# An FFT mixing layer fused with a two-layer MLP: another layout for the block transposes, later slots, another start

## The chip, the cores and the metric

The kernel runs on one core of a Trainium2 chip. The core's engines work side by side, each through its own list of instructions in order: TensorE (PE) for matrix products into PSUM, VectorE (DVE), ScalarE (ACT), GpSimd (POOL) and SyncE (SP); POOL and SP here mostly issue DMAs. The metric is the time of one execution on the device in microseconds (us), lower is better. Three runs of the kernel before took 919.62, 919.73 and 919.87 us.

## The reference

Each of 8 batches holds 3008 rows of 256 numbers. Along the rows it is transformed by a real FFT, multiplied by a filter of 1505 complex frequencies for each column, and transformed back. All 24064 rows then go through two dense layers with a leaky ReLU between them.

```python
X = np.fft.rfft(x, axis=1)                       # x: 8 x 3008 x 256
Y = X * (filt_r + 1j * filt_i)[None, :, :]       # 1505 x 256
y = np.fft.irfft(Y, n=x.shape[1], axis=1)
h = y.reshape(8 * 3008, 256) @ w_in              # 256 x 2048
g = np.maximum(0.01 * h, h)
out = g @ w_out                                  # 2048 x 256, float32
```

## The kernel before, in words

**The transform.** 3008 = 94 x 32 (`N1`, `N2`), so the FFT is done as two rounds of small products with constant matrices, with a transposition between them, and the same backwards. All operands are fp16. For one batch:

- *s1* (`s1_group`, 16 groups of two): for each of 32 values of n2, 94 rows of x meet a 94 x 128 matrix (`f1_sb`, twiddle factors included). The result is [128 frequencies, 32, 256]; ACT copies it from PSUM to the buffer `big` (line 205).
- *T1* (`turn`, four parts): DVE transposes 32 x 32 blocks, that is, it swaps the position within each group of 32 partitions with the index of n2 (line 212). It moves two fp16 numbers as one 32-bit element. A part covers 32 of the 128 such pairs in a row, with all 32 values of n2: 1024 elements a partition. In the buffer a row is laid out as (32, 256), so neighbouring elements of a block lie 512 B apart, in the source and in the destination.
- *s2* (`s2_group`, 12 groups): products with the 128 x 128 matrix `fwd2`, then the filter. In batch 0 (`split`), DVE makes two products y1, y2 and PE adds them in the next step. In the other batches DVE makes three products (lines 238 to 240) and POOL adds them (line 242).
- *sa* (`sa_group`): the inverse of s2, copied to `big` by ACT (line 255). *T2* (`turn`): the transposition back. *sb* (`sb_group`, 16 groups): products with `i1_sb`, which DVE copies into `yts` (line 272), already transposed for the dense layers.

Three `big` buffers go round; s1 of one batch, T1, sa and T2 write them in turn. All PSUM tiles of the transform (s1, s2, sa, sb) come from one pool, `pfp`, with two buffers, given out in the order of the program.

**The dense layers.** Rows are taken in 47 chunks of 512. A chunk has 8 slots. In a slot, `moe1_group` makes four products of 512 columns for 256 of the 2048 inner columns, and ACT writes their leaky ReLU (line 296); `moe2_slice` makes eight products of 256 columns for the chunk before (line 304). Every fourth slot the finished output, 128 x 512 in fp32, is copied from PSUM by DVE (line 308) and sent out by SP.

**The order.** It is written out by hand: nothing is moved by the framework, which only adds the waits that data and buffers need. Batch 0 is transformed ahead of everything else. The loop at the end then runs over 376 slots and 8 more; `plan` puts the transform groups of batches 1 to 7 into slots, behind the slot's `moe1_group` and ahead of its `moe2_slice`. Batch b starts at slot 47 (b - 1) - 8 (batch 1 at slot 0), and one batch is 47 slots of the dense layers. Within a batch: s1 in slots 0 to 7, T1 in 8 and 9, s2 from 11 on and sa from 15 on, each at 5/4 slots for a group, T2 in 30 and 31, sb in 32 to 39.

**The start.** SP issues the loads of the constants; POOL those of x, the filters, the weights and the next x, all of which turn fp32 into fp16 on the way. Each POOL DMA waits until the one eight places before it has landed. The filters are loaded into partitions 0 to 63 of `fa_sb` and `fb_sb`, and DVE copies them to 64 to 127, once as they are and once negated (lines 341, 342). One row of the filter (the highest frequency) overwrites a row of the copy by a DMA of its own (line 344). DVE also zeroes the three `big` buffers (line 190).

Of the kernel before, what the change touches and what calls it, by code (L numbers as in the profile page):

```python
# [23 lines left out]
def _build_np_constants(N):  # L24
# [68 lines left out]
    return (fwd1.astype(np.float16), inv1.astype(np.float16), small.astype(np.float16))  # L93
# [3 lines left out]
def kernel(  # L97
# [27 lines left out]
    f1_sb = cpool.tile([P, N2, P], FP16, name="f1_sb")  # L125
# [7 lines left out]
    big = [cpool.tile([P, Q, D], FP16, name=f"big{i}") for i in range(3)]  # L133
# [36 lines left out]
    def filt_load(dst, src):  # L170
        h = N2 // 2
        for s in range(2):
            q = s * Q
            nc.gpsimd.dma_start(dst[q : q + h], rows(src, NC * s, N1, 1, h, NC))

            nc.gpsimd.dma_start(
                dst[q + h : q + Q, 1 - s : NC - s],
                rows(src, N1 - (1 - s) - NC * s, N1, -1, h, NC - 1),
            )
        nc.gpsimd.dma_start(dst[h:Q, 0:1], rows(src, N1 // 2, N1, 1, h, 1))  # L180


    nc.sync.dma_start(f1_sb[:, 0:16, :], f1_d.ap()[:, 0:16, :])
    nc.sync.dma_start(f1_sb[:, 16:32, :], f1_d.ap()[:, 16:32, :])
# [13 lines left out]
    def s1_group(b, g):  # L198
        def go():
            ps = pfp.tile([P, 2, D], FP32, tag="pf", name=f"s1_b{b}_g{g}")  # L200
            for j in range(2):
                n2 = 2 * g + j
                nc.tensor.matmul(ps[:, j, :], f1_sb[:N1, n2, :], x_sb[:N1, n2, :],  # L203
                                 start=True, stop=True)
            nc.scalar.copy(big[(4 * b) % 3][:, ds(2 * g, 2), :], ps[:])  # L205
        return go

    def turn(src, dst, i, parts):
        w = D // 2 // parts
        a = src[:].bitcast(FP32)[:, :, ts(i, w)].rearrange("p n e -> p e n")  # L210
        o = dst[:].bitcast(FP32)[:, :, ts(i, w)].rearrange("p n e -> p e n")
        nc.vector.transpose(o, a)  # L212

# [5 lines left out]
    def s2_group(b, g, split):  # L219
        def go():  # L220
            src = big[(4 * b + 1) % 3]
# [7 lines left out]
            if split:  # L229
                y1 = ypp.tile([P, 2, D], FP16, tag="y", name=f"y1_b{b}_g{g}")  # L230
                y2 = ypp.tile([P, 2, D], FP16, tag="y2", name=f"y2_b{b}_g{g}")
                nc.vector.tensor_tensor(y1[:], ps[:], fa, AL.mult)
                nc.vector.tensor_tensor(y2[:], ps[:], fb, AL.mult)  # L233
                ys[(b, g)] = (y1, y2)
            else:
                p1 = scrp.tile([P, 2, D], FP32, tag="p1", name=f"p1_b{b}_g{g}")
                p2 = scrp.tile([P, 2, D], FP32, tag="p2", name=f"p2_b{b}_g{g}")
                nc.vector.tensor_tensor(p1[:], ps[:], fa, AL.mult)  # L238
                nc.vector.tensor_tensor(p2[0:64], ps[64:P], fb[64:P], AL.mult)  # L239
                nc.vector.tensor_tensor(p2[64:P], ps[0:64], fb[0:64], AL.mult)  # L240
                y1 = ypp.tile([P, 2, D], FP16, tag="y", name=f"y_b{b}_g{g}")
                nc.gpsimd.tensor_tensor(y1[:], p1[:], p2[:], AL.add)  # L242
                ys[(b, g)] = (y1,)
        return go

    def sa_group(b, g):
        def go():
# [7 lines left out]
            nc.scalar.copy(big[(4 * b + 2) % 3][:, ds(2 * g, 2), :], ps[:])  # L255
# [5 lines left out]
    def sb_group(b, g):  # L261
        dt, h = g % 2, g // 2

        def go():
            src = big[(4 * b + 3) % 3]
# [6 lines left out]
            nc.vector.tensor_copy(yv[:, :, ds(4 * h, 4)], ps[:].rearrange("p c a -> p a c"))  # L272
# [124 lines left out]
```

## Time and profile before

| | |
|---|---|
| Time, median of three runs | 919.73 us |
| The profiled execution's own time | 919.45 us |
| its span, first to last instruction | 917.6 us |
| mean granted TensorE clock | 0.972 of full speed |
| busy: PE, ACT, DVE, POOL | 799.3, 496.6, 464.6, 127.2 us |
| batch 0's transform alone, until the first dense product | 0 to 88.1 us |
| transposes (64) | 135.1 us busy on DVE |

A line of the page's groups reads: line of the kernel, engine, operation, what it writes <- what it reads, partitions x elements, count | busy us, mean ns of one | idle time of the engine before it, and what ended most of that. In the chain of waits and in the timeline, a line begins with its start and its duration in us. In the view by stretches a line gives the stretch, its length, the busy time of PE, weight loads, DVE, ACT and POOL with the number of instructions in brackets, then the granted clock, the share of the DMA engines and GB/s. Buffer numbers are left out of names: `s_b_g` is the PSUM tile of an s1 or s2 group, `sa_b_g`, `sb_b_g` those of sa and sb, `h_c_g` and `o_c_t` those of the two dense layers. The page's line on the granted clock and its neighbours (40 slices of the span):

```profile
PE   3065799889989898998989898998989898999998
DVE  5467386538650785329661676319661586400011
PEclk9999989999999998999999999999989999899999
```

### The profile page before, as it was taken

Reading aid. Unit: us, or ns where it says so; the run is one execution under the profiler, and the core shown is the slowest. Engines: PE = TensorE matmul, PEld = TensorE weight load, DVE = VectorE, ACT = ScalarE, POOL = GpSimd, SP = SyncE. Lnnn points to the kernel's source line nnn. Section 1 sums busy time; section 2 is a strip of 40 time slices with the busy share of each in tenths; the row PEclk is TensorE's granted clock in tenths of the full one; section 3 lists DMA queues with packets and bytes.
Section 4 is the critical chain, followed back from the end, with each engine's and each line's share of the span. In section 5 each row is a group of like instructions: output and inputs, shape, how many; then the busy total and the mean of one; then the engine's idle time right before and its main releaser. Section 6 shows DMA issues by size and latency. Waiting matters only on the chain.

```text
span 917.6 us, 13333 instructions
## 1 busy us (share of the span) xinstructions
PE 799.3 (87%) x5725; PEld 537.2 (59%) x5725; DVE 464.6 (51%) x571; ACT 496.6 (54%) x602; POOL 127.2 (14%) x123
## 2 busy tenths in 40 slices
PE   3065799889989898998989898998989898999998
PEld 1013456665667655785657655775656665667666
DVE  5467386538650785329661676319661586400011
ACT  4021756474637564585647565585636665455553
POOL 4100042003200240003300141003300041000000
PEclk9999989999999998999999999999989999899999
DMA  9900301041001400122101400013001001011011
GB/s 204 178 0 1 68 24 35 24 91 36 35 24 35 97 30 24 35 67 59 36 24 35 102 24 35 35 45 82 24 35 35 24 24 35 24 47 35 35 42 52
DMA packets 31707, 43.49 MB, mean 47 GB/s; under 512 B 2166, under 2 KB 29910, under 8 KB 30926
## 3 DMA queue, kind: packets, MB, share of 16 engines
q0 software_dynamic: 5504, 15.98, 10.3%
q1 hardware_dynamic: 26144, 26.66, 8.3%
q8 instruction: 45, 0.74, 0.4%
q14 instruction: 14, 0.11, 0.0%
HBM read 33.97 MB, written 24.64 MB: 64 GB/s over the span
## 4 chain that ended last, share of the span: by engine, by line
PE 68%; DVE 20%; DMA 4%; ACT 4%; issue 3%; POOL 0%; DVEq 0%; ACTq 0%; POOLq 0%
PE o_c_t L304 30%; PE h_c_g L291 28%; DVE big L212 12%; PE sb_b_g L269 3%; PE s_b_g L227 3%; DMA fa_sb<-in_filt_r_dram 3%; PE sa_b_g L253 2%; PE s_b_g L203 2%; DVE p_b_g L240 2%; DVE p_b_g L239 2%; DMA x_sb<-in_x_dram 2%; DVE p_b_g L238 2%; ACT gt_c L296 2%; ACT big L205 1%; DVE ost_c_t L308 1%
## 5 line engine op out<-in xcount | busy, mean ns | idle before, releaser
L296 ACT ACTIVATE gt_c<-h_c_g 128x1024 f16<-128x1024 f32 x376 | 385.8, 1026 | 355.9 <-PE h_c_g L291 355.1
L304 PE MATMUL o_c_t<-w_out_sb,gt_c 128*128 128x256 f16 x3008 | 398.5, 277 | 0.0
L291 PE MATMUL h_c_g<-yt,w_in_sb 128*128 128x512 f16 (+7 forms) x1728 | 396.4, 358 | 0.2 <-DVE yt L272 0.2
L304 PEld LDWEIGHTS <-gt_c 128*128 128x128 f16 x3008 | 295.2, 99 | 101.8 <-issue 18.4
L291 PEld LDWEIGHTS <-w_in_sb 128*128 128x128 f16 x1728 | 165.4, 99 | 99.4 <-issue 7.1
L308 DVE COPY ost_c_t<-o_c_t 128x512 f32<-128x512 f32 x94 | 64.9, 690 | 273.9 <-PE o_c_t L304 272.7
L212 DVE STREAM_TRANSPOSE big<-big 128x1024 f32<-128x1024 f32 x64 | 135.1, 2190 | 57.6 <-ACT big L205 47.7
L242 POOL TENSOR_TENSOR y_b_g<-p_b_g,p_b_g 128x512 f16<-128x512 f32 x84 | 106.6, 1269 | 256.6 <-DVE p_b_g L240 256.6
L272 DVE CAST yt<-sb_b_g 128x376 f16<-128x376 f32 x128 | 64.4, 545 | 58.4 <-PE sb_b_g L269 57.7
L255 ACT CAST big<-sa_b_g 128x512 f16<-128x512 f32 x96 | 55.8, 581 | 43.6 <-PE sa_b_g L253 43.6
L238 DVE TENSOR_TENSOR p_b_g<-s_b_g,fa_sb 128x512 f32<-128x512 f32 x84 | 57.9, 690 | 33.6 <-PE s_b_g L227 29.6
L205 ACT CAST big<-s_b_g 128x512 f16<-128x512 f32 x128 | 69.4, 605 | 5.0 <-PE s_b_g L203 4.8
L269 PE MATMUL sb_b_g<-i_sb,big 128*128 128x94 f16 x512 | 39.6, 223 | 34.6 <-DVE big L212 33.1
L269 PEld LDWEIGHTS <-big 128*128 128x128 f16 x512 | 32.9, 109 | 54.1 <-DVE big L212 37.0
L227 PE MATMUL s_b_g<-big,small_sb 128*128 128x512 f16 x88 | 36.4, 413 | 31.5 <-DVE y_b_g L233 17.3
L160 POOL DMA_DIRECT2D x_sb<-in_x_dram x22 | 11.7, 536 | 364.2 <-PE s_b_g L203 363.4
L239 DVE TENSOR_TENSOR p_b_g<-s_b_g,fb_sb 64x512 f32<-64x512 f32 x84 | 58.2, 692 | 1.1
L240 DVE TENSOR_TENSOR p_b_g<-s_b_g,fb_sb 64x512 f32<-64x512 f32 x84 | 57.4, 683 | 1.1
L203 PE MATMUL s_b_g<-x_sb,f_sb 94*128 94x256 f16 x256 | 43.7, 290 | 13.6 <-DMA x_sb<-in_x_dram 10.1
L253 PE MATMUL sa_b_g<-y_b_g,small_sb 128*128 128x512 f16 (+1 forms) x117 | 44.2, 414 | 1.3 <-ACT big L255 0.7
L203 PEld LDWEIGHTS <-f_sb 94*128 94x128 f16 x256 | 25.0, 102 | 29.2 <-issue 20.6
L225 PE MATMUL s_b_g<-big,small_sb 128*128 128x256 f16 x16 | 3.6, 317 | 33.0 <-DVE big L212 33.0
(27 smaller groups left out, 65.8 us busy)
## 6 DMA issues: line engine op xcount, KB each, us to landing
out_dram<-ost_c_t SPq DMA_DIRECT2D x94, 256.0 KB, 2.1
x_sb<-in_x_dram POOLq DMA_DIRECT2D x7, 1024.0 KB, 8.3
x_sb<-in_x_dram POOLq DMA_DIRECT2D x7, 480.0 KB, 10.8
f_sb<-fwd_const SPq DMA_DIRECT2D x2, 512.0 KB, 4.5
x_sb<-in_x_dram POOLq DMA_DIRECT2D x4, 256.0 KB, 9.5
w_in_sb<-in_moe_w_in_dram POOLq DMA_DIRECT2D x1, 1024.0 KB, 11.1
w_out_sb<-in_moe_w_out_dram POOLq DMA_DIRECT2D x1, 1024.0 KB, 14.9
i_sb<-inv_const SPq DMA_DIRECT2D x1, 752.0 KB, 12.0
```

What stands on the lines that cost most here:

```text
L203: nc.tensor.matmul(ps[:, j, :], f1_sb[:N1, n2, :], x_sb[:N1, n2, :], start=True, stop=True)
L205: nc.scalar.copy(big[(4 * b) % 3][:, ds(2 * g, 2), :], ps[:])
L212: nc.vector.transpose(o, a)
L238: nc.vector.tensor_tensor(p1[:], ps[:], fa, AL.mult)
L239: nc.vector.tensor_tensor(p2[0:64], ps[64:P], fb[64:P], AL.mult)
L240: nc.vector.tensor_tensor(p2[64:P], ps[0:64], fb[0:64], AL.mult)
L242: nc.gpsimd.tensor_tensor(y1[:], p1[:], p2[:], AL.add)
L269: nc.tensor.matmul(ps[:, j, :], src[:, n2, ts(dt, P)], i1_sb[:, n2, :], start=True, stop=True)
L291: nc.tensor.matmul(ph[:, j, ds(o, ln)], w_in_sb[:, dt, ts(ct, P)], yts[b % 2][:, dt, ds(lo, ln)], start=(dt == 0), stop=(dt == NDT - 1),)
L296: nc.scalar.activation(gts[ci][:, ds(2 * g, 2), :], ph[:], AF.Lrelu)
L304: nc.tensor.matmul(po[:, tj % 2, :], gts[ci][:, ct, ts(tj, P)], w_out_sb[:, ct, :], start=(ct == 0), stop=(ct == NCT - 1))
L308: nc.vector.tensor_copy(ost[:], po[:])
```

## The change

- **Layout.** A row of `big` is now (pair, n, 2) when s1 or sa has written it: ACT's copy (`spread`) interleaves two groups, writing four fp16 numbers (8 B) at a time, 128 B apart. `turn` reads 1024 contiguous elements and writes (n, pair) as before, at a step of 512 B. Matrix products read the same layout as before (`turned`).
- **Slots.** `plan` takes the places of T1, s2, T2 and sb and the step as arguments. sa now follows its s2 group by three slots, not four. Batch 1: T1 8, s2 11, T2 27, sb 30, one group a slot. Batches 2 to 7: T1 9, s2 13, T2 32, sb 36, 5/4 slots a group.
- **Engines.** The finished output is copied by ACT. In batch 0, sb's copies alternate between DVE and ACT.
- **Batch 0's middle part.** `s2_wide` makes four rows of products at once, in the PSUM pool of the first dense layer, and DVE's two products have 1024 elements instead of 512.
- **Loads.** `f1` has 94 rows instead of 128 and lies in memory in two contiguous halves. The filters are loaded and copied (`filt_copy`) in two halves of 12 columns; the first half's copies stand ahead of T1 on DVE, the second half's behind the first wide group. The row of the highest frequency is loaded into a tile of its own ahead of the filters and copied by DVE. Only one `big` buffer is zeroed. The statement that loads `i1` stands later.

```diff
@@ constants
+    fwd1 = fwd1[:N1].reshape(N1, 2, N2 // 2, P).transpose(1, 0, 2, 3)
@@ tiles
-    f1_sb = cpool.tile([P, N2, P], FP16, name="f1_sb")
+    f1_sb = cpool.tile([N1, N2, P], FP16, name="f1_sb")
+    fny_sb = cpool.tile([1, D], FP16, name="fny_sb")
-    big = [cpool.tile([P, Q, D], FP16, name=f"big{i}") for i in range(3)]
+    big = [cpool.tile([P, Q * D], FP16, name=f"big{i}") for i in range(3)]
@@ loads
+    def filt_copy(c0, c1):
+        nc.vector.tensor_copy(fa_sb[64:P, c0:c1, :], fa_sb[0:64, c0:c1, :])
+        nc.vector.tensor_scalar(out=fb_sb[64:P, c0:c1, :], in0=fb_sb[0:64, c0:c1, :],
+                                scalar1=-1.0, scalar2=None, op0=AL.mult)
+        if c0 == 0:
+            nc.vector.tensor_copy(fa_sb[64:65, 0, :], fny_sb[:])
+            nc.vector.memset(fb_sb[0:1, 0, :], 0.0)
+            nc.vector.memset(fb_sb[64:65, 0, :], 0.0)
...
+    nc.sync.dma_start(f1_sb[:, 0:H2, :], f1_d.ap()[0])
+    x_load(0, 4)
+    nc.sync.dma_start(f1_sb[:, H2:N2, :], f1_d.ap()[1])
     nc.sync.dma_start(small_sb[:], small_d.ap())
-    x_load(0, 4)
+    nc.gpsimd.dma_start(fny_sb[:], filt_r[N // 2 : N // 2 + 1, :])
+    for c0 in (0, HC):
+        filt_load(fa_sb, filt_r, c0, c0 + HC)
+        filt_load(fb_sb, filt_i, c0, c0 + HC)
...
-    for t in big:
-        nc.vector.memset(t[:], 0.0)
-    filt_load(fa_sb, filt_r)
-    filt_load(fb_sb, filt_i)
-    nc.sync.dma_start(i1_sb[:], i1_d.ap())
+    nc.vector.memset(big[2][:], 0.0)
@@ s1 (and the same in sa)
-            nc.scalar.copy(big[(4 * b) % 3][:, ds(2 * g, 2), :], ps[:])
+            spread(big[(4 * b) % 3], g, ps)
+    def spread(dst, g, ps):
+        o = dst[:].rearrange("p (e n t) -> p e n t", n=Q, t=2)[:, :, ds(2 * g, 2), :]
+        nc.scalar.copy(o, ps[:].rearrange("p n (e t) -> p e n t", t=2))
@@ turn
-        a = src[:].bitcast(FP32)[:, :, ts(i, w)].rearrange("p n e -> p e n")
-        o = dst[:].bitcast(FP32)[:, :, ts(i, w)].rearrange("p n e -> p e n")
+        a = src[:].bitcast(FP32)[:, ts(i, w * Q)].rearrange("p (e n) -> p e n", n=Q)
+        o = dst[:].bitcast(FP32).rearrange("p (n e) -> p e n", n=Q)[:, ts(i, w), :]
         nc.vector.transpose(o, a)
@@ s2 of batch 0
+    def s2_wide(b, g):
+        src = turned(big[(4 * b + 1) % 3])
+        ps = php.tile([P, 4, D], FP32, tag="ph", name=f"s2_b{b}_w{g}")
+        if g == 0:
+            for j in range(2):
+                nc.tensor.matmul(ps[:, j, :], fwd2(1 - j), src[:, j, :], start=True, stop=True)
+        for j in range(int(g == 0), 2):
+            nc.tensor.matmul(ps[:, ds(2 * j, 2), :], fwd2(0), src[:, ds(4 * g + 2 * j, 2), :],
+                             start=True, stop=True)
...
+        nc.vector.tensor_tensor(y1[:], ps[:], fa_sb[:, ts(g, 4), :], AL.mult)
+        nc.vector.tensor_tensor(y2[:], ps[:], fb_sb[:, ts(g, 4), :], AL.mult)
@@ sb, output
-            nc.vector.tensor_copy(yv[:, :, ds(4 * h, 4)], ps[:].rearrange("p c a -> p a c"))
+            copy(yv[:, :, ds(4 * h, 4)], ps[:].rearrange("p c a -> p a c"))
-            nc.vector.tensor_copy(ost[:], po[:])
+            nc.scalar.copy(ost[:], po[:])
@@ plan, and the order of batch 0
-    def plan(b, base):
+    def plan(b, base, t1, s2, t2, sb, step):
...
-            at(base + 8 + i // 2, t1_part(b, i))
+            at(base + t1 + i // 2, t1_part(b, i))
+            at(base + t2 + i // 2, t2_part(b, i))
         for g in range(12):
-            at(base + 11 + (5 * g) // 4, s2_group(b, g, False))
-            at(base + 15 + (5 * g) // 4, sa_group(b, g))
-        for i in range(4):
-            at(base + 30 + i // 2, t2_part(b, i))
+            at(base + s2 + (step * g) // 4, s2_group(b, g))
+            at(base + s2 + 3 + (step * g) // 4, sa_group(b, g))
         for g in range(16):
-            at(base + 32 + g // 2, sb_group(b, g))
+            at(base + sb + g // 2, sb_group(b, g, nc.vector.tensor_copy))
...
     x_load(1, 1)
+    filt_copy(0, HC)
     for i in range(4):
         t1_part(0, i)()
...
+    for g in range(6):
+        if g == 1:
+            filt_copy(HC, NC)
+        s2_wide(0, g)
+        if g >= 1:
+            sa_group(0, 2 * g - 2)(), sa_group(0, 2 * g - 1)()
     sa_group(0, 10)(), sa_group(0, 11)()
+    nc.sync.dma_start(i1_sb[:], i1_d.ap())
     for i in range(4):
         t2_part(0, i)()
     for g in range(16):
-        sb_group(0, g)()
-    for b in range(1, B):
-        plan(b, max(0, 47 * (b - 1) - 8))
+        sb_group(0, g, nc.scalar.copy if g % 2 else nc.vector.tensor_copy)()
+    plan(1, 0, 8, 11, 27, 30, 4)
+    for b in range(2, B):
+        plan(b, 47 * (b - 1) - 8, 9, 13, 32, 36, 5)
```

More of the change, by code (lines that the diff above doesn't have):

```diff
@@ L217, with s2_group @@
     ys = {}
-    def s2_group(b, g, split):
+    def s2_group(b, g):
         def go():
-            src = big[(4 * b + 1) % 3]
+            src = turned(big[(4 * b + 1) % 3])
             ps = pfp.tile([P, 2, D], FP32, tag="pf", name=f"s2_b{b}_g{g}")
@@ new lines, in go @@
+            ys[(b, g)] = (y1[:],)
+        return go
+    def s2_wide(b, g):
+        src = turned(big[(4 * b + 1) % 3])
+        ps = php.tile([P, 4, D], FP32, tag="ph", name=f"s2_b{b}_w{g}")
[5 more added lines that the diff above has]
+                             start=True, stop=True)
+        y1 = ypp.tile([P, 4, D], FP16, tag="yw1", bufs=2, name=f"y1_b{b}_g{g}")
+        y2 = ypp.tile([P, 4, D], FP16, tag="yw2", bufs=2, name=f"y2_b{b}_g{g}")
+        nc.vector.tensor_tensor(y1[:], ps[:], fa_sb[:, ts(g, 4), :], AL.mult)
+        nc.vector.tensor_tensor(y2[:], ps[:], fb_sb[:, ts(g, 4), :], AL.mult)
+        for j in range(2):
+            ys[(b, 2 * g + j)] = (y1[:, ts(j, 2), :], y2[:, ts(j, 2), :])
@@ L254, in go @@
                                      start=(i == 0), stop=(i == len(y) - 1))
-            nc.scalar.copy(big[(4 * b + 2) % 3][:, ds(2 * g, 2), :], ps[:])
+            spread(big[(4 * b + 2) % 3], g, ps)
         return go
```

59 lines of the change are left out of this document (21 added, 38 removed).

## Prediction, made before the run

> **What bounds the kernel now.** I read the page first, then the waits of TensorE (PE) in the main part alone, the chain of waits, the granted clock by stretch, and the start as a timeline.
>
> ```profile
> span 917.6 us, 13333 instructions
> PE 799.3 (87%) x5725; PEld 537.2 (59%) x5725; DVE 464.6 (51%) x571; ACT 496.6 (54%) x602; POOL 127.2 (14%) x123
> L308 DVE COPY ost_c_t<-o_c_t 128x512 f32<-128x512 f32 x94 | 64.9, 690 | 273.9 <-PE o_c_t L304 272.7
> L212 DVE STREAM_TRANSPOSE big<-big 128x1024 f32<-128x1024 f32 x64 | 135.1, 2190 | 57.6 <-ACT big L205 47.7
> L242 POOL TENSOR_TENSOR y_b_g<-p_b_g,p_b_g 128x512 f16<-128x512 f32 x84 | 106.6, 1269 | 256.6 <-DVE p_b_g L240 256.6
> L272 DVE CAST yt<-sb_b_g 128x376 f16<-128x376 f32 x128 | 64.4, 545 | 58.4 <-PE sb_b_g L269 57.7
> ```
>
> PE is the bound, but the program has two parts. Up to 88.09 us there is only batch 0's transform, one step after another. From there on (first product of the MoE) PE has work in nearly every slot. PE's waits after 88 us (who, for whom, us in total, times, longest):
>
> ```profile
> PE sb_b_g L269 <- DVE big L212: 24.4, 9, 3.9
> PE s_b_g L225 <- DVE big L212: 23.9, 7, 3.9
> PE s_b_g L227 <- DVE p_b_g L240: 8.8, 28, 0.4
> ```
>
> So 48.3 us are waits for the transposes, at two places in each of seven batches. What follows such a wait is in the chain (start, duration, what):
>
> ```profile
> 103.89 0.93 ACT gt_c L296
> 104.82 0.98 ACT big L205 x2
> 105.82 8.43 DVE big L212 x4
> 114.29 0.58 PE s_b_g L225 x2
> 114.87 1.71 PE o_c_t L304 x8
> 116.58 1.71 PE h_c_g L291 x4
> ...
> 119.98 0.86 PE h_c_g L291 x4
> 120.84 0.22 PE s_b_g L227
> 121.06 0.87 PE o_c_t L304 x8
> ```
>
> ```profile
> 391.85 0.44 PE s_b_g L203 x4
> ```
>
> After the wait the same twelve matmuls of a slot take 3.42 us instead of 1.73. The granted clock shows why (stretch, busy time of each engine, then the clock):
>
> ```profile
> 840.00:880.00 40.00, 40.00 (x279) 27.05 (x277) 4.15 (x6) 23.54 (x24) 0.00 (x0) 1.00 0.10 34
> 88.00:918.00 830.00, 765.89 (x5590) 523.00 (x5589) 410.71 (x516) 478.41 (x572) 112.89 (x96) 0.97 0.15 42
> ```
>
> ```profile
> 112.00:120.00 8.00, 5.71 (x24) 3.26 (x24) 6.23 (x8) 1.02 (x1) 1.26 (x1) 0.57 0.25 66
> ```
>
> ```profile
> core 0: 917.6 us, clock 0.972
> ```
>
> The mean clock of 0.972 is 25.7 us of lost clock over the span. Where no batch is transformed (840 to 880 us) PE is busy all the time at 1.00, so the loss belongs to the waits. PE was busy 766 of 830 us, so I count 92% of it, 23.6 us, as time.
>
> **The change, the main part.** A slot costs 0.87 + 0.86 = 1.73 us of PE, with two s1 groups 0.44 more, 2.17, and with one s2 and one sa group of 0.22 each as much. Batch 1's transposes start at 105.82; PE arrives at their reader at 110.40 (it waits until 114.29; longest wait 3.9). The new plan moves that reader, for batches 2 to 7, from three slots after s1 to five (the first transpose of a batch follows the last s1 evacuation, not its slot), and sb from three free slots after the last sa group to six. Batch 1 keeps three slots ahead of s2 and gets four ahead of sb.
>
> *A transpose that reads contiguous rows.* Before, source and destination both step 512 B per element; now only the destination does. No row has this form. Slope from two VectorE (DVE) rows: (690 - 545) / (512 - 376) = 1.07 ns per element, fixed part 145 ns. Lower bound: 1024 x 1.07 + 0.05 = 1.15 us back to back. Upper bound: nothing gained, 2.1 us. L272 speaks for the lower end: it reads single elements 376 B apart from PSUM and writes runs of 8 B, and lies on the same line as the plain copy L308 if its fixed part is the usual one; but it writes no single elements far apart. I take 1.15 us, so 4.6 us for four instead of 8.4.
>
> The Trainium skill (Advanced Engine Details and Errata, Memory Cachelines) says that an SBUF line is 16 bytes, that two hits on a line are needed to absorb the latency, and that another line at each access is penalised. By it the reads get four hits a line, but the writes still change line at each element; if that holds for writes, a transpose stays at about 2.1 us. No run here shows it; its time is that of the first rival below.
>
> With 4.6 us, batch 1's first wait ends (105.82 + 4.6 = 110.42 against 110.40), and all later ones have room: 5 x 1.73 = 8.7 us and 6 x 1.73 = 10.4 us. Removed: 48.3 us of waits and 23.6 us of clock.
>
> *What comes instead.* s2 and sa share two PSUM buffers. Where an s2 group gets the buffer of the s2 group one slot before, PE waits for three DVE products:
>
> ```profile
> 322.80 0.69 DVE p_b_g L238
> ...
> 324.95 0.39 PE s_b_g L227
> ...
> 325.43 0.13 DVE p_b_g L238
> ```
>
> 325.43 - 322.80 = 2.63 us against a slot of 2.17: 0.46 each. By the order of allocation this happens 4 times a batch now (28 waits in the row above). With sa at +3 slots it happens 5 times, and 9 times in batch 1, whose groups come every slot: 6 x 1 + 5 more, 11 x 0.46 = 5.1 us added. That sa comes one slot earlier is free: 0.39 + 3 x 0.69 + 1.27 (L242) is under 4 us, three slots are over 5.
>
> *Evacuations on ScalarE (ACT).* Output copies: 94 x 0.69 leave DVE, where no product waited for them long, and join ACT at about 0.5 us back to back (half of 0.98 for two of that size). ACT's fullest slots are those of s1: 0.93 + 0.98 + 0.5 / 4 = 2.03 us against PE's 2.17. Hidden; behind a waiting output copy stands the next slot's Lrelu, which needs a later PE group anyway. The interleaved writes (`spread`: runs of four fp16, 128 B apart) are in no row. Lower bound: as now, 0.49 back to back (L272's 8-byte runs cost DVE nothing extra). Upper bound: a transpose's present price per element, 2.1 ns x 512 = 1.1 us. I take 0.49.
>
> Main part: 48.3 + 23.6 - 5.1 = **66.8 us less**.
>
> **The change, the start.** DVE and POOL (its DMA issues) in order of time, then the us from issue to landing:
>
> ```profile
> 14.55 0.49 POOL L180 DMA_DIRECT2D fa_sb<-in_filt_r_dram  x1 [1.63 <-DMA x_sb<-in_x_dram]
> 20.07 0.49 POOL L180 DMA_DIRECT2D fb_sb<-in_filt_i_dram  x1 [0.82 <-DMA fa_sb<-in_filt_r_dram]
> 20.31 8.30 DVE L212 STREAM_TRANSPOSE big<-big 128x1024 f32<-128x1024 f32 x4 [6.24 <-ACT big L205]
> 28.64 1.75 DVE L341 COPY fa_sb<-fa_sb 64x6144 f16<-64x6144 f16 x1
> 30.68 1.48 POOL L344 DMA_DIRECT2D fa_sb<-in_filt_r_dram  x1 [5.40 <-DVE fa_sb L341]
> 45.57 0.69 DVE L232 TENSOR_TENSOR y_b_g<-s_b_g,fa_sb 128x512 f16<-128x512 f32 x1 [13.04 <-DMA fa_sb<-in_filt_r_dram]
> ```
>
> ```profile
> fa_sb<-in_filt_r_dram POOLq DMA_DIRECT2D x1, 8.0 KB, 8.6
> fb_sb<-in_filt_i_dram POOLq DMA_DIRECT2D x1, 8.0 KB, 8.6
> ```
>
> The 0.5 KB row of L344 was queued behind weights and the next x, and the first product waited for it to 45.57. It is now loaded ahead of the filters. In the chain the rest runs like this:
>
> ```profile
> 46.26 0.60 DVE y_b_g L233
> ...
> 51.48 0.59 PE s_b_g L227
> 52.06 0.87 PE sa_b_g L253 x2
> ...
> 70.91 8.30 DVE big L212 x4
> ...
> 80.31 0.49 PE sb_b_g L269 x4
> ...
> 88.09 1.90 PE h_c_g L291 x4
> ```
>
> Step by step, after:
> 1. The first transpose now stands behind `filt_copy` of the first half on DVE, and that behind its loads. Half of the filter bytes (all of fa) landed at 14.55 + 8.6 = 23.2, all at 28.7; the new first half is as many bytes, in ten issues instead of five. `f1` is 94 rows instead of 128, so I take 22.3. Then half of 1.75 for the copy of fb and 0.6 for the small ones: transposes start at 23.8 instead of 20.3. If the halves landed no earlier than the whole, it would be 30.
> 2. Four transposes: 28.4.
> 3. Six wide groups: first matmuls 0.9; twelve DVE products of 1024 elements, by the slope 0.60 + 512 x 1.07 = 1.15 each, 13.8; second `filt_copy` 1.9. PE needs six matmuls of about 0.43 (0.87 for two) for a group, 2.6 against DVE's 2.3: four groups, 1.4. Last sa pair and evacuation 2.4. Sum 20.4, end at 48.8 (now 25.3 us from 45.57 to 70.91).
> 4. Four transposes: 53.4.
> 5. sb: now 79.2 to 88.09. With alternating engines each of the two buffers still goes through four matmuls (0.49), one evacuation (0.55, L272) and the semaphores, so 8.8 again. MoE from 62.3.
>
> Two memsets of `big` fall away; they ended long before the transposes, free. The later place of the i1 load changes nothing: SP has nothing to wait for ahead of it. On POOL's queue nine more issues of about 0.5 us stand ahead of the weights and the next x; those landed by 45.5 (L344's row came last), so now by about 50, before 62. Start: 88.1 - 62.3 = **25.8 us less**.
>
> **Sum.** 917.6 - 66.8 - 25.8 = 825.0 us of span. Around it lie 919.45 - 917.6 = 1.85, and the profiled run is 0.28 under the median of 919.73: 827.1, so **827 us**.
>
> **Rivals.**
> *Transposes stay at 2.1 us.* For it: the writes keep their 512 B step; against it: the price now is about twice the slope, which one strided side can explain. Start 2 x 3.7 = 7.4; batch 1's first wait stays, 3.9 + 1.7 of clock, and its second is 8.3 + 0.7 - 4 x 1.73 = 2.1 + 1.7; later batches have room (8.7 and 10.4 us). Sum 16.8: **844 us**.
>
> *Interleaved evacuation dear.* At 1.1 us back to back an s1 slot is 0.93 + 0.12 + 2.2 = 3.25 on ACT, 1.08 over PE's 2.17, in 48 slots: 52; batch 1's eight slots, which ACT already sets, 8 x (2.2 - 0.98) = 10; start 4. **893 us**. At 0.65 it is 12 us: 839. For it: no such row on ACT; against it L272.
>
> *Slower.* The same place, at a price at which it eats all: 48 x (1.05 + 2S - 2.17) + 8 x (2S - 0.98) + 7 = 92 gives S = 1.31 us, 2.7 times now. At four times ACT's slope between these rows, (0.93 - 0.49) / 512 = 0.86 ns, S is 1.8 us: 119 + 21 + 14, and some 20 in sa slots: **1001 us**. No row shows an engine at that rate.
>
> *The new loads gate the start.* First half landing with the whole: 6 us, **833 us**; more, smaller issues speak for it.
>
> **How the numbers follow.** Forecast, with loads up to 6 us late, 0.63 (own range 815 to 838). Transposes unchanged 0.22. Dear evacuation, still faster, 0.09; beyond 1.31 us 0.02. Left: 0.04, half of it below 815. The range 814 to 860 leaves out the upper dear evacuations, the slower case and half of the rest, about 0.12; unknown costs on top of rival one are in it. What a measurement can tell from no change is 0.2%, 1.8 us: faster 0.97, same 0.01, slower 0.02.
>
> **What would show it.** Transposes: L212's successor at 1.15 or 2.1 us. Plan: waits of PE for DVE after the start near zero and a clock over 0.99. `spread`: ACT CAST still near 0.6 us. Start: first transpose at about 24 us, first MoE matmul at about 62. PE waits for DVE products near 12 us instead of 8.8. Wrong would be: a half-speed clock without long waits, or ACT as releaser in s1 slots.

## The result, and the profile after

The changed kernel takes **861.68 us** (861.0 to 862.45), the kernel before 919.67 beside it on the same chip: ratio 0.937, 95% interval 0.936 to 0.939. That is 58 us less, where 93 were forecast, and 1.7 us above the range.

The page of the kernel after: span, the engines' busy time, then the rows of the groups that the change touches (ACT's evacuations of s1 and sa, and the output copies).

```profile
span 860.4 us, 13332 instructions
PE 775.4 (90%) x5725; PEld 528.4 (61%) x5725; DVE 372.5 (43%) x458; ACT 547.6 (64%) x704; POOL 130.4 (15%) x131
L230 DVE STREAM_TRANSPOSE big<-big 128x1024 f32<-128x1024 f32 x64 | 116.2, 1929 | 192.2 <-ACT big L224 192.1
L224 ACT CAST big<-s_b_g 128x512 f16<-128x512 f32 x128 | 69.9, 614 | 27.1 <-PE s_b_g L216 27.1
L224 ACT CAST big<-sa_b_g 128x512 f16<-128x512 f32 x96 | 55.5, 581 | 27.6 <-PE sa_b_g L284 27.6
L339 ACT COPY ost_c_t<-o_c_t 128x512 f32<-128x512 f32 x94 | 55.5, 591 | 18.3 <-PE o_c_t L335 13.7
```

TensorE (PE) lost 23.9 us of busy time: 19.1 in the main part (765.9 to 746.8), where the granted clock rose from 0.97 to 0.99, and 4.8 in the start. The mean granted clock rose from 0.972 to 0.986, but the two means don't compare as they stand. The trace's records of the clock begin at 92.1 us before the change and at 65.3 after it, and the mean counts what lies ahead of them as full speed; so only the mean after the change contains a stretch at half speed in the start, from 72.2 to 92.7 us. The transposes fell only from 2190 to 1929 ns. From the chain of waits of the kernel after (start, duration, what), the first and second transposes of the start and the first product of the MoE:

```profile
46.52 7.09 DVE big L230 x4
...
72.13 7.09 DVE big L230 x4
...
88.12 1.87 PE h_c_g L322 x4
```

The MoE begins at 88.12 us; before it began at 88.09. **The start gained nothing**, where 25.8 us were forecast. That it comes out at nothing is chance: T1, the first round of transposes, starts 26.2 us later than before (46.52 against 20.31), and the stretch from there to T2 is 25.0 us shorter (25.6 against 50.6). All 57.2 us of span (917.6 to 860.4) come from the main part, where 66.8 were forecast. PE's waits there, after 88 us:

```profile
PE s_b_g L248 <- DVE p_b_g L254: 15.7, 38, 0.7
PE s_b_g L246 <- DVE big L230: 2.7, 1, 2.7
PE s_b_g L248 <- ACT big L224: 1.4, 1, 1.4
```

Of 48.3 us of waits for transposes one wait of 2.7 is left, batch 1's ahead of s2; waits for VectorE's (DVE) products grew from 8.8 to 15.7, and one wait of 1.4 us for ACT is new.

Why the start didn't move stands in the timelines of the kernel after. PE first: start, duration, instruction, and in brackets the idle time before it with what ended it.

```profile
19.87 1.03 PE L216 MATMUL s_b_g<-x_sb,f_sb 94*128 94x256 f16 x4 [19.87 <-DMA f_sb<-fwd_const]
...
32.26 1.04 PE L216 MATMUL s_b_g<-x_sb,f_sb 94*128 94x256 f16 x4 [7.52 <-DMA f_sb<-fwd_const]
...
53.65 0.59 PE L266 MATMUL s_b_w<-big,small_sb 128*128 128x256 f16 x2 [16.52 <-DVE big L230]
```

DVE in the same stretch:

```profile
37.48 0.17 DVE L204 MEMSET fa_sb<- 32x128 uint32 x1 [37.48 <-DMA fa_sb<-in_filt_r_dram]
39.49 0.17 DVE L205 MEMSET fb_sb<- 32x128 uint32 x1 [1.84 <-DMA fb_sb<-in_filt_i_dram]
40.55 3.47 DVE L206 MEMSET big<- 128x4096 uint32 x1 [0.90 <-DMA fb_sb<-in_filt_i_dram]
44.06 0.95 DVE L186 COPY fa_sb<-fa_sb 64x3072 f16<-64x3072 f16 x1
```

Two things are late that the prediction did not look at. The matrix `f1` arrives at 19.9 and 32.3 us, one half after the other. And the memsets, which the diff writes behind the filter loads, wait for these loads at the head of DVE's queue; ahead of T1 stand then 3.47 us for `big` and the filter's first copy.

The DMA rows of the kernel after, against one row of the kernel before in the second fence (size, then median us from issue to landing; `f_sb` has no landing here):

```profile
f_sb<-fwd_const SPq DMA_DIRECT2D x2, 376.0 KB
fa_sb<-in_filt_r_dram POOLq DMA_DIRECT2D x6, 96.0 KB, 10.2
small_sb<-small_const SPq DMA_DIRECT2D x1, 192.0 KB, 31.6
```

```profile
f_sb<-fwd_const SPq DMA_DIRECT2D x2, 512.0 KB, 4.5
```

Both halves are issued within the first 1.5 us of the span; the halves of 94 rows were waited for until 19.9 and 32.3 us, where the larger ones of 128 rows landed 4.5 us after issue. In the trace's semaphore records the semaphore of a 94-row load rises in 3 steps, that of `small` (128 rows) in 16. The Trainium skill (DMA: Bandwidth & Descriptors, Why a DMA increments its semaphore by 16 and not by 1) says that a load spreads over the largest number of engines up to 16 that divides the size of its outer dimension, that each of these raises the semaphore by one, and that the issuing sequencer adds the rest at once. 94 is 2 x 47: two engines and one step for the rest, three steps. The trace agrees: the steps come at 1.17, 19.70 and 19.82 us for the first half, at 1.57, 32.00 and 32.21 for the second. Other loads were late with them: `small` took 31.6 us, a filter piece of 96 KB 10.2. The same records show how. 14 of `small`'s 16 steps come by 4.4 us, the last two at 32.9 and 33.1, behind the second half of `f1`; the first load of x, on POOL's queue, has 14 by 6.2 us and two at 9.9 and 10.3. So a load over all 16 engines is held up by its shares on two of them, which fits the two that carry `f1`.

### The profile page after: what moved, and what is told of

It is laid out like the page before. It is cut to its first block, busy times and chain, and to the rows that moved or that the text cites. A ratio compares the mean times of both kernels' runs of the same rounds, so it can differ in the third digit from the quotient of the medians.

```text
span 860.4 us, 13332 instructions
## 1 busy us (share of the span) xinstructions
PE 775.4 (90%) x5725; PEld 528.4 (61%) x5725; DVE 372.5 (43%) x458; ACT 547.6 (64%) x704; POOL 130.4 (15%) x131
## 4 chain that ended last, share of the span: by engine, by line
PE 72%; DVE 19%; DMA 4%; issue 2%; ACT 2%; POOL 1%; DVEq 0%; ACTq 0%; POOLq 0%
PE o_c_t L335 32%; PE h_c_g L322 31%; DVE p_b_g L253 5%; DVE p_b_g L252 5%; DVE p_b_g L254 4%; PE sb_b_g L300 3%; PE s_b_g L216 3%; DVE big L230 2%; PE s_b_g L248 2%; DMA fb_sb<-in_filt_i_dram 2%; DMA x_sb<-in_x_dram 2%; PE sa_b_g L284 1%; ACT big L224 1%; ACT gt_c L327 1%; DVE y_b_g L273 1%
## 5 line engine op out<-in xcount | busy, mean ns | idle before, releaser
L335 PE MATMUL o_c_t<-w_out_sb,gt_c 128*128 128x256 f16 x3008 | 389.3, 273 | 0.0
L322 PE MATMUL h_c_g<-yt,w_in_sb 128*128 128x512 f16 (+7 forms) x1728 | 388.9, 353 | 0.3 <-DVE yt L303 0.3
L335 PEld LDWEIGHTS <-gt_c 128*128 128x128 f16 x3008 | 290.8, 98 | 107.3 <-issue 27.3
L230 DVE STREAM_TRANSPOSE big<-big 128x1024 f32<-128x1024 f32 x64 | 116.2, 1929 | 192.2 <-ACT big L224 192.1
L303 DVE CAST yt<-sb_b_g 128x376 f16<-128x376 f32 x120 | 60.7, 545 | 79.9 <-PE sb_b_g L300 79.9
L339 ACT COPY ost_c_t<-o_c_t 128x512 f32<-128x512 f32 x94 | 55.5, 591 | 18.3 <-PE o_c_t L335 13.7
L284 PE MATMUL sa_b_g<-y_b_g,small_sb 128*128 128x512 f16 (+1 forms) x117 | 41.4, 388 | 4.2 <-DVE y_b_g L273 2.7
L248 PE MATMUL s_b_g<-big,small_sb 128*128 128x512 f16 x77 | 29.1, 378 | 17.1 <-DVE p_b_g L254 15.7
L300 PE MATMUL sb_b_g<-i_sb,big 128*128 128x94 f16 x512 | 35.3, 215 | 9.9 <-DVE big L230 7.6
L284 PEld LDWEIGHTS <-small_sb 128*128 128x128 f16 x117 | 11.5, 102 | 21.4 <-issue 5.9
```

Source lines behind the costliest of these rows:

```text
L284: nc.tensor.matmul(ps[:, ds(*js), :], m(sp), t[:, ds(*js), :], start=(i == 0), stop=(i == len(y) - 1))
L300: nc.tensor.matmul(ps[:, j, :], src[:, n2, ts(dt, P)], i1_sb[:, n2, :], start=True, stop=True)
L322: nc.tensor.matmul(ph[:, j, ds(o, ln)], w_in_sb[:, dt, ts(ct, P)], yts[b % 2][:, dt, ds(lo, ln)], start=(dt == 0), stop=(dt == NDT - 1),)
L335: nc.tensor.matmul(po[:, tj % 2, :], gts[ci][:, ct, ts(tj, P)], w_out_sb[:, ct, :], start=(ct == 0), stop=(ct == NCT - 1))
```

## The experiments

**1. f1 in 64 + 30 rows** (`f1_split`). Nothing else changes.

```diff
-    nc.sync.dma_start(f1_sb[:, 0:H2, :], f1_d.ap()[0])
+    for lo, hi in ((0, 64), (64, N1)):
+        nc.sync.dma_start(f1_sb[lo:hi, 0:H2, :], f1_d.ap()[0][lo:hi])
...
-    nc.sync.dma_start(f1_sb[:, H2:N2, :], f1_d.ap()[1])
+    for lo, hi in ((0, 64), (64, N1)):
+        nc.sync.dma_start(f1_sb[lo:hi, H2:N2, :], f1_d.ap()[1][lo:hi])
```

> The changed kernel with one edit: the two loads of f1 (94 rows) are issued as 64 and 30 rows each. Theory A (two separate faults in the start: the 94-row loads land at 19.9 and 32.3 us and hold up s1 and the loads beside them; and DVE's three memsets stand behind the filter loads and hold up the first transpose until 46.5 us): f1 lands by about 7 us, s1 ends near 20, the filters land near 29 as in the kernel before, but the memsets still wait for them; transposes start at about 29 + 0.4 + 3.5 + 2.4 = 35 us, so about 11 us less than 861.7: 850. Rival B (nineteen small POOL loads in place of ten, each waiting for the one eight places earlier, are what is late): the filters still land near 39 us, transposes start near 46, time within 2 us of 861.7.

Measured: **848.63 us** (848.49 to 849.68), ratio 0.923 [0.919, 0.926] to before, 13.1 us less than the changed kernel. The DMA rows of this run:

```profile
f_sb<-fwd_const SPq DMA_DIRECT2D x2, 256.0 KB, 5.3
fa_sb<-in_filt_r_dram POOLq DMA_DIRECT2D x6, 96.0 KB, 5.4
small_sb<-small_const SPq DMA_DIRECT2D x1, 192.0 KB, 9.4
```

All three are back under 10 us, the filter pieces too, which the edit does not touch. So the 94-row loads alone cost 13 us. (The kernel already loads x, of 94 rows too, as 64 and 30.)

**2. The memsets ahead of the filter loads** (`zero_first`), f1 as in the changed kernel.

```diff
+    nc.vector.memset(fa_sb[Q : 2 * Q, NC - 1 : NC, :], 0.0)
+    nc.vector.memset(fb_sb[Q : 2 * Q, NC - 1 : NC, :], 0.0)
+    nc.vector.memset(big[2][:], 0.0)
     nc.gpsimd.dma_start(fny_sb[:], filt_r[N // 2 : N // 2 + 1, :])
...
-    nc.vector.memset(fa_sb[Q : 2 * Q, NC - 1 : NC, :], 0.0)
-    nc.vector.memset(fb_sb[Q : 2 * Q, NC - 1 : NC, :], 0.0)
-    nc.vector.memset(big[2][:], 0.0)
```

> The changed kernel with one edit: the three memsets on DVE are written ahead of the filter loads. Theory A: the first transpose then waits for s1 (its last evacuation ends at 37.8 us in the changed kernel) and for the copies of the first filter half (landed at 36.4, copied at about 38), so it starts near 38 instead of 46.5: 853. If the memsets did not matter it stays at 861.7. Rival B makes no difference here: its loads are as late as before.

Measured: **852.7 us** (850.9 to 853.57), ratio 0.927 [0.924, 0.930]: 9 us less.

**3. Both** (`both_loads`).

> Both edits, f1 as 64 and 30 rows and the memsets ahead of the filter loads. Theory A: this is the start that the prediction had in mind, first transpose at about 24 us, 22.5 us less than 861.7: 839. The two edits give more together (22) than added up (11 + 8.5), because each alone leaves the other gate. Rival B: the first half of the filters lands at 33 to 36 us whatever f1 does, transposes start near 36: 851.

Measured: **838.67 us** (838.01 to 838.78), ratio 0.912 [0.909, 0.914]. The gains nearly add: 23.0 us for both, 13.1 and 9.0 alone; that each edit alone would leave the other gate standing, as was expected, shows in 0.9 us at most. T1 in the DVE timelines of the three runs, in the order 1, 2, 3:

```profile
34.01 7.07 DVE L232 STREAM_TRANSPOSE big<-big 128x1024 f32<-128x1024 f32 x4
```

```profile
38.10 7.08 DVE L230 STREAM_TRANSPOSE big<-big 128x1024 f32<-128x1024 f32 x4
```

```profile
25.11 7.08 DVE L232 STREAM_TRANSPOSE big<-big 128x1024 f32<-128x1024 f32 x4
```

With both mended, T1 starts at 25.1 us, where the prediction had 23.8. The runs that follow, up to the last three, are this kernel with one thing altered.

**4. What a strided side costs a transpose** (`turn_forms`). Each batch transposes in another form; `near` is contiguous, `far` at a step of 512 B, `a` the source and `o` the destination. Batches 5 and 6 write at steps of 528 and 516 B, batch 7 at 16 B.

```diff
+        a, o = near_a, far_o
+        if b == 1:
+            a, o = far_a, far_o
+        elif b == 2:
+            a, o = far_a, near_o
+        elif b == 3:
+            a, o = near_a, near_o
+        elif b in PITCH:
...
```

> Built on the kernel with both edits. It measures the transpose by itself: each batch from 1 to 7 uses another access pattern in both of its transpositions, with the same number and size of instructions, so the output is not the reference's from batch 1 on. Batch 1: source and destination at a step of 512 B (as before the change). Batch 2: source at 512 B, destination contiguous. Batch 3: both contiguous. Batch 4: source contiguous, destination at 512 B (the change). Batch 5 and 6: source contiguous, destination at 528 and 516 B. Batch 7: source contiguous, destination at 16 B. Theory W (the step of the writes is what still costs): batch 3 takes 1.15 us back to back, batch 4 1.77, batch 1 2.08, batch 2 between 1.15 and 1.77; batch 7 shows whether a step of one line already costs it. Rival: a transpose has a price of its own near 1.77 that no step changes, then batch 3 is at 1.77 as well. Rival: 512 B is a bad step by its power of two, then batches 5 and 6 are well under batch 4.

Measured: 841.78 us in one run. The first four transposes of each batch from 1 to 7 in the DVE timeline (batch 4 has the changed kernel's form, source contiguous and destination at 512 B):

```profile
82.32 8.46 DVE L253 STREAM_TRANSPOSE big<-big 128x1024 f32<-128x1024 f32 x4 [17.68 <-ACT big L226]
...
174.01 7.47 DVE L253 STREAM_TRANSPOSE big<-big 128x1024 f32<-128x1024 f32 x4 [20.03 <-ACT big L226]
...
270.22 4.62 DVE L253 STREAM_TRANSPOSE big<-big 128x1024 f32<-128x1024 f32 x4 [23.46 <-ACT big L226]
...
366.66 7.32 DVE L253 STREAM_TRANSPOSE big<-big 128x1024 f32<-128x1024 f32 x4 [23.66 <-ACT big L226]
...
462.67 7.65 DVE L253 STREAM_TRANSPOSE big<-big 128x1024 f32<-128x1024 f32 x4 [23.45 <-ACT big L226]
...
558.93 7.62 DVE L253 STREAM_TRANSPOSE big<-big 128x1024 f32<-128x1024 f32 x4 [23.49 <-ACT big L226]
...
655.16 7.62 DVE L253 STREAM_TRANSPOSE big<-big 128x1024 f32<-128x1024 f32 x4 [23.45 <-ACT big L226]
```

Four contiguous transposes take 4.62 us; with one strided side, whichever, 7.3 to 7.7; with both 8.46. The step itself does not matter: 16 B costs what 512, 516 and 528 do. So the side that is made contiguous first brings the smaller gain, 8.46 to 7.32 here, and the larger one, 7.32 to 4.62, comes only when the second follows; the change stopped at the first.

**5. The layout undone** (`old_layout`): evacuation and transposes as before, slots new.

```diff
-        nc.scalar.copy(o, ps[:].rearrange("p n (e t) -> p e n t", t=2))
+        nc.scalar.copy(turned(dst)[:, ds(2 * g, 2), :], ps[:])
...
-        a = src[:].bitcast(FP32)[:, ts(i, w * Q)].rearrange("p (e n) -> p e n", n=Q)
+        a = src[:].bitcast(FP32).rearrange("p (n e) -> p e n", n=Q)[:, ts(i, w), :]
```

> On the kernel with both start edits (838.7 us), the interleaved layout alone is taken back: s1 and sa are copied plainly, and a transpose reads and writes at a step of 512 B. Theory (the layout is worth what the measured prices say, 2.1 against 1.75 us a part): start 2 x 1.3 = 2.6 us more; batch 1's wait ahead of s2 grows from 2.7 by 1.3, its wait ahead of sb by about 1.3; batches 2 to 7 hide 8.4 us behind five and six slots. Sum 5 us: 844. ScalarE's copies take the same time. Rival (the interleaved copy costs ScalarE something that the plain one does not): less than 841.

Measured: **845.58 us** (844.13 to 846.42), ratio 0.919 [0.918, 0.921]. The waits for transposes in the main part, and ACT's plain evacuation:

```profile
PE s_b_g L247 <- DVE big L231: 3.9, 1, 3.9
...
PE sb_b_g L301 <- DVE big L231: 1.2, 1, 1.2
```

```profile
L225 ACT CAST big<-s_b_g 128x512 f16<-128x512 f32 x128 | 70.1, 616 | 10.1 <-PE s_b_g L218 10.1
```

With the new slots the layout is worth 6.9 us, or 5.4 of span between the two profiled executions (842.1 against 836.7). In the start, two rounds of four transposes are each 8.3 - 7.1 = 1.2 us longer (with T1 1.0 us earlier and the wide groups 0.3 shorter in this run, the MoE begins only 1.1 later, at 68.10 against 66.98). In the main part batch 1 waits 3.9 - 2.7 = 1.2 us more ahead of s2 and 1.2 ahead of sb, and one more stretch of 3.41 us is at half speed, 1.7 us of lost clock; the rest is in none of these rows. The interleaved evacuation costs nothing: 614 ns against 616.

**6. The slots undone** (`old_slots`), layout new.

```diff
-    plan(1, 0, 8, 11, 27, 30, 4)
-    for b in range(2, B):
-        plan(b, 47 * (b - 1) - 8, 9, 13, 32, 36, 5)
+    for b in range(1, B):
+        plan(b, max(0, 47 * (b - 1) - 8), 8, 11, 30, 32, 5)
...
-            at(base + s2 + 3 + (step * g) // 4, sa_group(b, g))
+            at(base + s2 + 4 + (step * g) // 4, sa_group(b, g))
```

> On the kernel with both start edits, the slots alone are taken back: T1 8, s2 11, sa four slots behind s2, T2 30, sb 32 in every batch, 5/4 slots a group. Theory (the later slots took away the waits, whatever the transposes cost): waits of about 2.2 us come back at both places of batches 2 to 7 and ahead of sb in batch 1, 13 x 2.2 = 29, with half-speed stretches behind some of them, up to 10; fewer waits for DVE's products give 7 back. 860 to 871. Rival (the faster transposes took them away): under 845.

Measured: **855.46 us** (853.22 to 856.38), ratio 0.930 [0.928, 0.932], below what was expected. The waits are there:

```profile
PE s_b_g L248 <- DVE big L232: 14.4, 7, 2.7
PE sb_b_g L302 <- DVE big L232: 11.7, 7, 1.7
PE s_b_g L250 <- DVE p_b_g L256: 8.4, 28, 0.3
```

What did not come is the lost clock: the core's mean stays at 0.988, against 0.990 in the third run, and the clock records show one stretch of 3.41 us at half speed behind these 14 waits. Waits of about 2 us mostly leave the clock alone; the last section shows why.

**7. Both undone** (`both_old`), with edits 5 and 6 together.

> Both start edits (838.67 us), with the layout and the slots of the kernel before together; the output copies stay on ScalarE. With the layout alone undone it was 845.58 us, with the slots alone 855.46 us: if the two edits simply added, this would be 838.7 + 6.9 + 16.8 = 862 us. Theory: they don't add, because each alone already makes the waits short enough that TensorE mostly keeps its full clock; together undone the waits come back at 3.4 to 3.9 us, twice in each of seven batches, 46 to 49 us in all, the clock falls behind them again (mean 0.975 or less), and the time is 885 to 900 us. Rival: the lost clock of the kernel before belonged to VectorE's output copies and not to the waits; then the waits return but the clock stays near 0.988, and the time is 868 to 880 us.

Measured: **891.56 us** (889.86 to 893.88), ratio 0.969 [0.966, 0.973]. The waits, and the core's span and clock:

```profile
PE s_b_g L247 <- DVE big L231: 23.1, 7, 3.9
PE sb_b_g L301 <- DVE big L231: 20.1, 7, 2.9
```

```profile
die 0 (median of its cores): 890.8 us, clock 0.962
```

Together the two edits are worth 891.6 - 838.7 = 52.9 us. The new slots alone bring 46.0 of them (run 5), the new layout alone 36.1 (run 6), so the one that comes second adds only 6.9 or 16.8. Two things lie behind this. The waits for transposes don't add themselves: 43.2 us with both undone, 26.1 and 5.1 with one, 2.7 with none, because the room that the slots give hides the longer transposes as well. And the clock falls with both undone: eleven stretches at half speed in the main part, 44.4 us together, against one of 3.41 us in each of runs 5 and 6 and none in the third run. DVE's output copies are not in this kernel, so they are not what costs the clock.

**8. sa one slot later in batches 2 to 7** (`sa_later`), **9. output copies back on DVE** (`ost_dve`).

```diff
-            at(base + s2 + 3 + (step * g) // 4, sa_group(b, g))
+            at(base + s2 + (3 if b == 1 else 4) + (step * g) // 4, sa_group(b, g))
```

```diff
-            nc.scalar.copy(ost[:], po[:])
+            nc.vector.tensor_copy(ost[:], po[:])
```

> On the kernel with both start edits, sa follows s2 by four slots again in batches 2 to 7 (batch 1 unchanged). Theory (the two PSUM buffers: with three slots, five s2 groups of a batch get the buffer of the s2 group just before them, with four slots only four, as in the kernel before): a batch's slots of s2 lose about 3.0 - 1.9 = 1.1 us, six batches 6.6 us: 832, and the waits of PE for DVE's products fall from 15.6 to about 10. Rival (DVE's pace of 2.07 us a group sets these slots): no change.

> On the kernel with both start edits, the output copies go back from ScalarE to DVE. Theory: ScalarE had room (2.03 us of 2.17 in the s1 slots), so it wins nothing there, at most the 0.1 us of slots that now take 2.22 to 2.34; on DVE a copy stands behind the transposes (up to 3.5 us at a time) and adds 0.69 to the three products, so some slots of s2 get longer: 1 to 5 us more, 840 to 844. Rival (ScalarE became too full with these copies): faster than 838.

Measured: **831.24 us** (829.4 to 832.75), ratio 0.904 [0.902, 0.906], and **842.81 us** (841.58 to 843.82), ratio 0.916 [0.915, 0.918]. The waits for products in the two runs, 15.6 in 38 in the third run:

```profile
PE s_b_g L250 <- DVE p_b_g L256: 9.7, 32, 0.3
```

```profile
PE s_b_g L250 <- DVE p_b_g L256: 19.6, 38, 1.2
```

So the sa lag of three slots in batches 2 to 7, part of the change, costs 7.4 us, and moving the output copies to ACT gains 4.1: with copies on DVE single waits grow to 1.2 us.

**10 to 12. What was left on the path** (`best1`, `best2`, `best3`). `best1` puts T1 ahead of the filter's first copy, gives sb of the start a second PSUM pool, lets DVE evacuate batch 1's odd s1 groups, and spreads the later batches so that no two s2 groups in a row share a PSUM buffer. The last argument of `plan` is now sa's lag. `best2` and `best3` change only sb's slots: two groups a slot again (`g // 2`), all groups of dt=0 first, batch 1 from slot 31, and batches 2 to 7 from slot 38 in `best2` and 39 in `best3`.

```diff
-    plan(1, 0, 8, 11, 27, 30, 4)
+    plan(1, 0, 8, 12, 27, 32, 4, 3)
...
-        plan(b, 47 * (b - 1) - 8, 9, 13, 32, 36, 5)
+        plan(b, 47 * (b - 1) - 8, 9, 13, 35, 40, 6, 5)
...
-            at(base + sb + g // 2, sb_group(b, g, nc.vector.tensor_copy))
+            at(base + sb + (7 * g) // 16, sb_group(b, g, nc.vector.tensor_copy))
```

> The kernel with both start edits (838.67 us) and later sa groups (831.24 us), and beside them every part that the earlier runs left on the path is moved: the first T1 stands ahead of the filter's first copy on VectorE, the start's sb groups go all dt=0 first and use a second PSUM pool, batch 1's odd s1 groups are evacuated by VectorE, and in batches 1 to 7 s2, T2 and sb are spread further (sa lag 5 slots), so that two s2 groups in a row never share a PSUM buffer. Theory: what is left in the main part are waits for VectorE's products (9.7 us, 32 times, in the run with later sa groups), the first T1's wait (2.7 us) and the ACT-bound first slots (about 3.5 us), and in the start the sb groups (about 5 us) and the copy ahead of T1 (about 2 us): 831 - 9 - 2.7 - 3.5 - 5 - 2 = about 809 us, range 800 to 818, with waits for p of under 3 us in all. Rival: the waits for p come from VectorE's total load in each batch and not from which groups stand next to each other; then they stay near 10 us and the time is 817 to 822 us. Second rival: a later T2 and sb make slots wait for their sb groups, and the time is 825 us or more, with the waits in MoE's first product of a batch.

> The kernel of 815.85 us with sb's slots changed alone: all groups of dt=0 first, which need only the first two parts of T2, so that sb starts two slots earlier in batches 2 to 7 (one in batch 1) and has two groups a slot in eight slots instead of up to three in seven. Theory: the new waits of PE for sb's evacuation (yt) in that run, 6.5 us in 14 waits of at most 0.5 us, come from the third group of a slot, which needs the PSUM buffer of the first; they go, and the time is 808.5 to 811 us. Rival: they come from VectorE's evacuation itself being late behind T2; then they stay near 6.5 us, in fewer and longer waits, and the time is 814 to 818 us, or more if the dt=0 groups now wait for T2.

> The run before, with sb of batches 2 to 7 one slot later (39 instead of 38), still two groups a slot. In that run the 6.5 us of waits for sb's evacuation were gone, and in their place stood 10.1 us in 6 waits for T2 (1.7 us each): the second product of the first dt=0 group waited for the last part of T2, so a half of T2 is not enough for it. One slot (1.74 us) later T2 has ended. Theory: both kinds of wait are then gone, 818.4 - 10.1 = 808 us, range 806 to 811. Rival: the two-group slots 39 to 46 now reach into the next batch's s1 and give waits there; then 812 to 816 us.

Measured: **815.85 us** (814.76 to 816.63), ratio 0.887 [0.885, 0.889]; **818.38 us** (817.12 to 819.03), ratio 0.891 [0.889, 0.893]; **807.95 us** (807.49 to 808.27), ratio 0.878 [0.875, 0.881]. PE's waits in the main part that differ, one fence for each run in this order:

```profile
PE sb_b_g L306 <- DVE yt L309: 6.5, 14, 0.5
PE s_b_g L250 <- DVE p_b_g L256: 2.4, 8, 0.3
```

```profile
PE sb_b_g L306 <- DVE big L232: 10.1, 6, 1.7
```

```profile
PE s_b_g L250 <- DVE p_b_g L256: 2.4, 8, 0.3
PE s_b_g L250 <- ACT big L226: 1.4, 1, 1.4
PE s_b_g L248 <- DVE big L232: 0.5, 1, 0.5
```

In `best1` the waits for products went as expected, and sb's third group in a slot brought a new wait of 0.46 us on average (6.5 in 14), for a PSUM buffer. `best2` removed that and ran into T2: the expectation that dt=0 needs only half of T2 was wrong, the first group waited for the last part. One slot later, in `best3`, both are gone; 4.3 us of waits are left in the 745 us from 60 us on. This version beats both kernels. `best1` alters several things at once, and these runs don't tell what each is worth.

## Why the prediction was wrong

**The step that failed is step 1 of the start** ("`f1` is 94 rows instead of 128, so I take 22.3 ... transposes start at 23.8"). It took fewer rows as less work. T1 started at 46.5, 22.7 us late. Runs 1 to 3 show the two causes, both in the diff: the row count that two engines carry (13.1 us), and the memsets' new place behind the loads (9.0 us). "Two memsets of `big` fall away ... free" looked at what is removed and not at where the third now stands. With both mended the time is 838.7, and step 1 is off by 1.3 us (T1 at 25.1).

**The transposes were mis-sized** ("I take 1.15 us"): 7.1 to 7.2 us for four instead of 4.6. The slope from two plain copies was right for what it describes, contiguous rows (4.62 in run 4); the mistake was to give the whole excess to the side that the change removes. The row L272 wrote runs of 8 B and could say nothing of single far elements, as the text itself noted. Weighing against it was the rule that the prediction cited from the Trainium skill (Advanced Engine Details and Errata, Memory Cachelines), with the doubt whether it holds for writes. Run 4 agrees with it for writes at every step that it has, from 16 B on (7.3 to 7.7 us for four, against 4.62 contiguous); but a read-side gain is there too, so its time (2.1 us) was too high. This cost 5.0 us in the start's two rounds, and batch 1's wait of 2.7 us, which the prediction had ending exactly in time ("110.42 against 110.40").

**Waits for products**: the count was right (28 + 11 = 39 forecast, 38 found), the price a little low: 8.8 + 5.1 = 13.9 us against 15.7. The sa lag was mis-sized. The prediction called one slot earlier "free" and counted one more shared buffer a batch for it, 6 x 0.46 = 2.8 us; run 8 shows 7.4 us, and six waits fewer with 5.9 us less in them, about 1 us each.

**The sum closes.** From 827.1 to 838.7, the time with both causes mended, are 11.6 us: 5.0 (transposes in the start) + 1.3 (step 1) - 1.6 (the wide groups: T2 of the third run starts at 51.01 in its chain of waits, 51.01 - 25.11 - 7.09 = 18.8 instead of 20.4) + 2.7 (batch 1) + 1.8 (products) = 9.2; 2.4 us are left over. Of these 2.1 are clock: PE's busy time in the main part fell from 765.9 to 744.4 us in the third run, by 21.5 where the prediction took 23.6. From 838.7 to 861.7 are the 23.0 us of runs 1 to 3.

**Right**: sb of the start 8.85 us (79.27 to 88.12), 8.8 forecast; no wait for a transpose after batch 1; `spread` free; the output copies hidden on ACT. The **clock** came back nearly whole: before, the clock records show eleven stretches at half speed from 92.1 us on, 51.2 us together, and after the change one of 3.41 us, behind batch 1's wait. The mean of 0.986 stays under the 0.99 that the prediction named as a sign, because it contains the start's stretch from 72.2 to 92.7 us. As time, the clock was worth less than counted: PE's busy time in the main part fell by 19.1 us, where 23.6 were forecast.

**The rivals**: "the new loads gate the start" named the right place, but with filters a few us late (833), not with `f1` and memsets. "Transposes stay at 2.1" was half right. The upper end of the range, 860, was made for that rival and the dearer evacuations; that the time lies so near to it is chance, since its largest miss is in the start. The dear evacuation and the slower case fell with 614 ns.

## What to carry to other kernels

The row count of a load that SP issues decides how many DMA engines carry it (94 rows: two), and other loads wait for those engines; so look at each changed size as a product of factors before costing it by bytes. When a strided operand moves from one side of an instruction to the other, price each side by itself, and expect the rest to stay. When an instruction moves in the program, ask what its engine's queue then has to wait for ahead of it. Two edits that shorten the same wait need not add, in the wait or in the clock behind it: undo each alone, and both together.

## What the runs showed of the hardware

- **A strided side of a 32x32 block transpose** of 128x1024 fp32 costs about 0.7 us, be it source or destination, and the destination at 16 B as much as at 512 B; both sides cost about 0.95 us, not 1.4 (from run 4, a quarter of 7.32, 8.46 and 4.62).
- **A load on two engines holds up loads on sixteen**: with the 94-row `f1` a filter piece took 10.2 us instead of 5.4 and `small` 31.6 instead of 9.4; of `small`'s 16 steps 14 had come by 4.4 us.
- **The clock behind a wait.** In the changed kernel and in the third run batch 1's wait is the same, 2.69 us, and what follows is not. PE's timeline of the changed kernel, then of the third run:

```profile
113.25 0.59 PE L246 MATMUL s_b_g<-big,small_sb 128*128 128x256 f16 x2 [2.69 <-DVE big L230]
113.62 1.92 PE L335 MATMUL o_c_t<-w_out_sb,gt_c 128*128 128x256 f16 x8
```

```profile
91.44 0.38 PE L248 MATMUL s_b_g<-big,small_sb 128*128 128x256 f16 x2 [2.69 <-DVE big L232]
91.66 1.03 PE L337 MATMUL o_c_t<-w_out_sb,gt_c 128*128 128x256 f16 x8
```

The eight products take 1.92 us in one and 1.03 in the other. The Trainium skill (TensorE: Matmul & The Clock Gate, Part 1: The HAM clock gate) says that activity is judged in windows of about 3.4 us that run freely, whatever the kernel does. The traces agree, and they show what decides. In their records of the granted clock all stretches that end within the run last whole multiples of 3.41 us. In the changed kernel 2.57 us of the wait fall into one such window (109.72 to 113.13 us), and in the next the granted clock is 0.50; in the third run the same wait falls into two, with 1.15 and 1.54 us, and the clock stays at 1.00.

The traces of all 14 runs, from 70 us on, hold 3098 such windows at full speed. In the 29 that a stretch at half speed follows PE is idle for 1.92 us or more; in the other 3069 it is idle for at most 1.98 us. So what costs clock here is not a wait's length but its share of one window: some 2 us of 3.41. Waits of 2.7 us did and did not (runs 1 and 2 did, 6 did not), and in the kernel before one of 3.73 us, at 622.6 us, cost none, since it fell half and half into two windows. Where a wait falls was not steered in any run; it differed by itself.
